# Windowed attention and a mixture of experts on one core: chunks of 4, 6, 7 and 7 tiles instead of four batches of 6, and a first attention written anew

## The chip, the cores and the metric

The kernel runs on one NeuronCore of a Trainium2 chip. The metric is the device time of one execution in microseconds (us); the kernel before takes 1218.8 us (median of three runs). The core has five engines that run side by side, each with its own queue in order: TensorE (PE) multiplies matrices into PSUM, VectorE (DVE) and ScalarE (ACT) work on elements, GpSimd (POOL) too but without access to PSUM, and SyncE (SP) issues most transfers (DMA). They wait for each other through semaphores.

## The reference

Attention for 4 batches, 8 heads, 768 positions and 64 numbers per head, and then a mixture of 4 experts over the 3072 rows, each weighted by a row's probability for it:

```
pos = np.arange(S); rel = pos[:, None] - pos[None, :]
is_global = pos[None, :] < n_global                 # 8
is_local = (rel >= 0) & (rel < n_local)             # 96
dist = np.where(is_global & ~is_local, float(n_local), np.abs(rel))
scores = q @ k.T / sqrt(D) - slopes[:, None, None] * dist
scores = np.where(is_global | is_local, scores, -1e9)
a = np.exp(scores - scores.max(-1)); a /= a.sum(-1) + 1e-9
x = (a @ v).transpose(0, 2, 1, 3).reshape(B * S, H * D)      # 3072 x 512
p = probs / (probs.sum(-1) + 1e-9)
out = sum(p[:, e:e+1] * (np.maximum(x @ w1[e], 0) @ w2[e]) for e in range(4))
```

w1[e] is 512 x 1024 and w2[e] is 1024 x 512. A query needs only the 95 keys before its own, its own, and the first eight.

## The kernel before

A tile is 128 rows of a batch, so a batch has six. Heads go in pairs, since two heads of 64 numbers fill 128 partitions; "a tile-pair" below is one tile for one pair of heads, and there are 96. The window of a tile is 256 keys: 96 of the tile before, 32 at the front of the batch, and its own 128. The first tile of a batch needs its own 128 alone.

**Attention.** `load` fetches q, k and v of a pair with both heads side by side. PE transposes q and k (`transpose_half`: three tiles into PSUM tile `pt`); copies bring them to SBUF. `windows` makes `vg`, v shifted to the windows' first halves. A step then takes one tile-pair a stage further (`flow`): `scores` (two matmuls, one for each head, into `ps`); `softmax`, where DVE adds the bias `nbias` and finds the maximum in one instruction (in profiles CUSTOM_DVE_ANT_0), ACT takes the exponential with the sum `zsum`, and the weights `pb` are scaled by 1/`zsum`; `turn`, where PE transposes `pb` into `pt` and ACT copies it to `pT`; and, for three tiles at once, `weigh`, where PE multiplies with v and vg, head j into 64 rows of `px`, and ACT copies `px` to `x`.

There are two forms of it. The first batch has nothing beside it (`early=True`): q lies in `early_q` with the other head's rows filled with zeros, so that a score matmul uses all 128 rows, in full float32. Later batches run beside the experts: q is split into a high and a low part (`st_q`), laid out by DMA into `qd`, k likewise into `kd`, and two fp32r matmuls per head give the scores.

**Experts.** They run batch by batch, and in a batch by unit: expert e and a quarter g of its 1024 hidden columns, 16 units to a batch. `first(i)` makes the hidden part `h` by Strassen's scheme in Winograd's form: seven products of half-size blocks, which need the blocks and sums B11, B21, B22, T1 to T4 of x (`blocks`; `xB` and `xT` in profiles) and the blocks and sums of w1 (`w1s`). Every operand is a high and a low part, so a product is six matmuls of half a batch's rows, 384 columns. `second(i)` multiplies each tile of `h` with `w2s`, six matmuls of 512 columns, and DVE adds the result, times the row's probability, to `acc`. PSUM tiles of both are `pm`, of which there are four.

**Weights.** Unit i's `raw1` and `raw2` are loaded by SP, POOL makes four sums, ACT copies the high parts and POOL subtracts for the low ones (`load_w1`, `load_w2`). One buffer each for `raw1`, `raw2` and `sums`, two for `w1s` and `w2s`. In the first batch they are also written to memory (`keep`), and in later batches fetched from there (`fetch`).

**Order.** The main loop emits `first(0)`, `first(1)`, `second(0)`, `first(2)`, and so on. After each product or tile it takes a step of the waiting `chores` (the weights of unit i+2, the blocks of the next batch) and as many steps of the next batch's attention as keep it evenly spread. While `Ordered.on` is set, each engine keeps the order of the code; that holds for the first attention and the first seven products. Later a scheduler in the build chooses each engine's order. The first attention is spread in the same way with the weights of units 0 and 1, and with half of the blocks of x (`blocks(0, (0,), po)`).

## Time and profile before

| What | us |
|---|---|
| runs of the kernel | 1215.73 to 1218.8, median 1218.8 |
| span of the profiled execution | 1215.1 |
| PE busy | 1176.1 |
| DVE busy | 824.0 |
| ACT busy | 499.9 |
| POOL busy | 214.1 |
| first matmul of the experts begins | 81.20 |

The profile gives no time of its own for the profiled execution beside its span, so sums are made against 1215.1, which is by the lower of the three runs. The page's slices show how the span divides (40 slices of 30 us; busy tenths, and the granted clock of PE in tenths):

```profile
PE   6789999999999999999999999999999999999997
DVE  5667657767668776766768766676676766666664
ACT  4874556555642453444442344444443211111110
POOL 5465565465541000000002000000000100000000
PEclk9989999999999999999999999999999999999999
```

POOL is busy for the first 380 us, in the first attention and while the weights are split. All recorded calls pass one helper, so every row has the line L42: read them by the names of the tiles. PE and PEld are two rows of one engine, the matmuls and the loads of their stationary operand; recorded times of successive matmuls overlap, so the price of one is read from start to start.

### The profile page before, as it was taken

The page shows a single profiled execution, that of the slowest core. Times are in us where ns is not written, and L with a number is a line of the kernel's source. Part 1 is how long each engine was busy: PE and PEld are TensorE (multiplying, and loading weights), DVE is VectorE, ACT ScalarE, POOL GpSimd, SP SyncE. Part 2 cuts the span into 40 slices and gives each one's busy share as a digit, 9 for nine tenths or more (in the row PEclk, how much of TensorE's full clock was granted, in tenths as well). Part 3 has the DMA queues.
Part 4 walks back from the last instruction along what each step waited for, and adds up shares of the span by engine and source line. Part 5 has one row for each costly group of instructions (what it writes and reads, how often), then busy time and mean ns, then how long its engine had stood idle before and what let it go on. Part 6 is the DMA issues. An engine that isn't in the chain of part 4 may idle for free.

```text
span 1215.1 us, 18027 instructions
## 1 busy us (share of the span) xinstructions
PE 1176.1 (97%) x6624; PEld 1053.3 (87%) x6624; DVE 824.0 (68%) x1778; ACT 499.9 (41%) x1284; POOL 214.1 (18%) x226
## 2 busy tenths in 40 slices
PE   6789999999999999999999999999999999999997
PEld 4568788998998899899898999899899899999996
DVE  5667657767668776766768766676676766666664
ACT  4874556555642453444442344444443211111110
POOL 5465565465541000000002000000000100000000
PEclk9989999999999999999999999999999999999999
DMA  6427978778777757575646856665663655555532
GB/s 161 123 107 218 306 241 275 263 246 308 261 281 251 226 183 225 193 223 199 216 155 218 275 189 205 211 202 192 204 205 142 238 195 191 186 181 182 184 128 88
DMA packets 122705, 251.40 MB, mean 207 GB/s; under 512 B 83184, under 2 KB 91376, under 8 KB 106224
## 3 DMA queue, kind: packets, MB, share of 16 engines
q1 hardware_dynamic: 118864, 243.87, 60.3%
q10 hardware_dynamic: 3744, 6.30, 1.4%
q8 instruction: 54, 0.88, 0.3%
q14 instruction: 43, 0.35, 0.1%
HBM read 174.11 MB, written 52.43 MB: 186 GB/s over the span
## 4 chain that ended last, share of the span: by engine, by line
PE 86%; ACT 4%; DMA 3%; DVE 3%; POOL 2%; issue 2%; SPq 0%; ACTq 0%; POOLq 0%; DVEq 0%
PE pm L42 76%; PE pt L42 6%; PE ps L42 3%; ACT pb L42 2%; DMA raw<-in_moe_w_dram 2%; POOL sums L42 1%; POOL w2s L42 1%; DVE pb L42 1%; PE px L42 1%; DMA qd<-st_q 1%; SPq L42 0%; ACT pT L42 0%; DVE early_q L42 0%; ACT xT L42 0%; DVE x L42 0%
## 5 line engine op out<-in xcount | busy, mean ns | idle before, releaser
L42 PE MATMUL pm<-w2s,h 128*128 128x512 f32 x2304 | 551.6, 393 | 4.5 <-DVE h L42 4.4
L42 PEld LDWEIGHTS pm<-w2s,h 128*128 128x128 f32 x2304 | 426.0, 188 | 92.5 <-DVE h L42 6.5
L42 DVE SCALAR_TENSOR_TENSOR acc<-pm,prob,acc 128x512 f32<-128x512 f32 x360 | 268.1, 749 | 148.7 <-PE pm L42 146.5
L42 PE MATMUL pm<-xT,w1s 128*128 128x384 f32 x1536 | 296.5, 338 | 0.2 <-ACT xT L42 0.2
L42 PEld LDWEIGHTS pm<-xT,w1s 128*128 128x128 f32 x1536 | 267.7, 189 | 2.3 <-issue 1.4
L42 PE MATMUL pm<-xB,w1s 128*128 128x384 f32 x1152 | 226.7, 338 | 1.8 <-DVE xB L42 1.5
L42 PEld LDWEIGHTS pm<-xB,w1s 128*128 128x128 f32 x1152 | 201.2, 188 | 7.0 <-DVE xB L42 1.9
L42 ACT ACTIVATE h<-pm 128x384 fp32r<-128x384 f32 x256 | 124.7, 490 | 178.0 <-DVE pm L42 174.7
L42 DVE SCALAR_TENSOR_TENSOR h<-pm,h 128x384 fp32r<-128x384 f32 x256 | 140.7, 552 | 13.3 <-ACT h L42 9.8
L42 ACT ACTIVATE pb<-pb,nmax 128x256 f32<-128x256 f32 (+1 forms) x192 | 93.1, 487 | 108.2 <-DVE nmax L42 107.5
L42 ACT COPY p<-pm 128x384 f32<-128x384 f32 x64 | 30.6, 477 | 190.8 <-PE pm L42 190.6
L42 POOL COPY vg<-v 32x768 f32<-32x768 f32 x16 | 13.1, 821 | 498.4 <-DMA v<-in_v_dram 495.6
L42 DVE TENSOR_TENSOR u<-pm,p 128x384 f32<-128x384 f32 x64 | 35.6, 556 | 73.7 <-PE pm L42 55.0
L42 ACT ACTIVATE pb<-pb,zsum 128x256 f32<-128x256 f32 (+1 forms) x168 | 74.8, 484 | 18.1 <-DVE zsum L42 18.1
L42 DVE CUSTOM_DVE_ANT_0 pb<-ps,nbias 128x256 f32<-128x256 f32 (+1 forms) x192 | 71.4, 395 | 9.0 <-PE ps L42 4.4
L42 ACT COPY pT<-pt 128x512 f32<-128x512 f32 (+1 forms) x96 | 52.4, 546 | 56.6 <-PE pt L42 56.4
L42 DVE TENSOR_TENSOR pm<-pm,vv 128x384 f32<-128x384 f32 x128 | 71.6, 559 | 1.6 <-PE pm L42 1.4
L42 PE MATMUL pt<-ident,pb 128*128 128x128 f32 x352 | 58.6, 280 | 12.7 <-ACT pb L42 6.3
L42 PEld LDWEIGHTS pt<-ident,pb 128*128 128x128 f32 x352 | 43.3, 143 | 23.1 <-ACT pb L42 14.3
L42 DVE TENSOR_TENSOR vv<-pm,u 128x384 f32<-128x384 f32 x64 | 35.6, 557 | 27.3 <-PE pm L42 26.5
L42 DVE TENSOR_TENSOR u<-pm,u 128x384 f32<-128x384 f32 x64 | 35.6, 557 | 25.3 <-PE pm L42 24.6
L42 POOL TENSOR_TENSOR w2s<-raw,w2s 128x512 fp32r<-128x512 f32 x32 | 41.0, 1295 | 57.9 <-ACT w2s L42 57.7
(88 smaller groups left out, 895.7 us busy)
## 6 DMA issues: line engine op xcount, KB each, us to landing
w1s<-kept SPq DMA_DIRECT2D x48, 1792.0 KB, 7.2
w2s<-kept SPq DMA_DIRECT2D x48, 1024.0 KB, 4.8
kept<-w1s SPq DMA_DIRECT2D x16, 1792.0 KB, 9.6
qd<-st_q SPq DMA_DIRECT2D x96, 192.0 KB, 4.8
raw<-in_moe_w_dram SPq DMA_DIRECT2D x32, 512.0 KB, 5.9
kept<-w2s SPq DMA_DIRECT2D x16, 1024.0 KB, 6.8
v<-in_v_dram SPq DMA_DIRECT2D x16, 384.0 KB, 3.6
out_dram<-acc ACTq DMA_DIRECT2D x24, 256.0 KB, 3.3
```

What stands on the lines that cost most here:

```text
L42: ins = fn(*args, **kwargs)
```

## The change

The 24 tiles of all batches are cut into chunks of 4, 6, 7 and 7 (`SIZES`), and experts and attention go by chunk. A chunk's attention is done in segments that do not cross a batch and have at most four tiles: one of 4; 2 and 4; 2, 4 and 1; 1, 4 and 2. A segment that begins within a batch also loads and turns the tile of keys before it and tile 0 (`tiles_of_keys`), in shorter runs and so in more transfers. The seven products of a unit have 256, 384, 448 and 448 columns. Weights are split in chunks 0 and 1 (`KEEP = 1`), written to memory in chunk 1 and fetched in chunks 2 and 3.

The first attention (four tiles of four pairs, 16 steps instead of 24) is written by itself. q stays without zeros, and a head's score matmul uses its own 64 rows. Scores of two tiles are made together. `pb` is not scaled: the eight sums of a pair stay in PSUM (`z`), DVE makes `zr` = 1/(z + 1e-9), PE turns it by eight small matmuls (`pt<-ident,zr`) and spreads it over 64 rows each, ACT copies that to `rT`, and DVE multiplies the products with v by it when it takes them out of PSUM. The copies to `pT` go from ACT to DVE, the copies of q to ACT alone; k goes to ACT for the first pair and to DVE later. The blocks of x are made in two parts in a new order (`raw_first`), and unit 0 takes its products in that order.

```
+    SIZES = (4, 6, 7, 7)
+    SEG = 4
+    KEEP = 1
+    def tiles_of_keys(t0, t1):
+        return list(range(t1)) if t0 < 2 else [0] + list(range(t0 - 1, t1))
...
+    def first_attention(A):
...
+        def scores(pr, g):
+            ps = A.ps.tile([P, 2, 4 * P], F32, name="ps")
...
+                for j in range(2):
+                    own = slice(j * D, (j + 1) * D)
+                    te.matmul(
+                        ps[:, j, 2 * i * P : 2 * i * P + m],
+                        got["q"][own, t * P : (t + 1) * P],
+                        got["k"].rearrange("p t c -> p (t c)")[own, c0 : c0 + m],
+                        start=True, stop=True,
+                    )
...
+        def sums(pr):
+            zr = A.small.tile([P, SEG, 2], F32, name="zr")
+            ve.tensor_scalar_add(zr, psum[pr]["z"], 1e-9)
+            ve.reciprocal(zr, zr)
+            rt = A.pt.tile([P, 512], F32, name="pt")
+            for i in range(n):
+                for j in range(2):
+                    te.matmul(
+                        rt[j * D : (j + 1) * D, i * P : (i + 1) * P],
+                        zr[:, i, j : j + 1].to_broadcast([P, D]),
+                        ident, start=True, stop=True,
+                    )
+            rT = A.rT.tile([P, 512], F32, name="rT")
+            ac.copy(rT, rt)
...
+        def finish(pr):
+            ve.tensor_mul(x[:, pr, :], psum[pr]["px"], psum[pr]["rT"])
...
+        for s in range(last + 3):
+            m, t = divmod(s, n)
+            if s <= last:
+                softmax(steps[s])
...
+            if t == 0 and m:
+                sums(PAIRS[m - 1])
+            if 1 <= s <= last + 1:
+                turn(A, steps[s - 1], ve.tensor_copy)
+            if s >= 2:
+                weigh(psum[steps[s - 2]["pr"]]["px"], steps[s - 2])
+                if t == 1 and m:
+                    finish(PAIRS[m - 1])
+            if m < NPAIR:
+                if t == 0:
+                    scores(PAIRS[m], 1)
+                if m + 1 < NPAIR:
+                    if t == 0:
+                        prepare_q(PAIRS[m + 1])
+                    if t == 1:
+                        prepare_k(PAIRS[m + 1], ve.tensor_copy)
+                    if t == 2:
+                        scores(PAIRS[m + 1], 0)
+                if t == 2 and m + 2 < NPAIR:
+                    start(PAIRS[m + 2])
...
-        if b > 0:
+        if c > KEEP:
             wts[(i, 1)] = fetch("w1s", (e, g, 1), [P, 2, 7, 2, P], lambda t: {
...
-        waiting[(i, 1)] = (e, g, 1), dst
+        if c == KEEP:
+            waiting[(i, 1)] = (e, g, 1), dst
...
-                chores.append(load_w1(i + 2, 9) if fn is first else load_w2(i + 2))
+                chores.append(load_w1(i + 2, 6) if fn is first else load_w2(i + 2))
```

PE in the first attention, before, from the end of the first three tiles of a pair (`ps` scores, `pt<-ident,pb` the turned weights, `px` products with v):

```order
L42 MATMUL pt<-ident,pb 128x128 x4
L42 MATMUL px<-pT,v 64x128 x2
L42 MATMUL px<-pT,vg 64x128 x2
L42 MATMUL px<-pT,v 64x128 x2
L42 MATMUL px<-pT,vg 64x128 x2
L42 MATMUL px<-pT,v 64x128 x2
L42 MATMUL pt<-ident,q 128x128 x3
L42 MATMUL ps<-early_k,early_q_165 128x256 x2
L42 MATMUL pt<-ident,pb 128x128 x4
```

The same place now, around the end of the first pair:

```order
L42 MATMUL pt<-ident,pb 128x128 x4
L42 MATMUL px<-pT,vg 64x128 x2
L42 MATMUL px<-pT,v 64x128 x2
L42 MATMUL pt<-ident,zr 64x128 x8
L42 MATMUL pt<-ident,pb 128x128 x4
L42 MATMUL px<-pT,vg 64x128 x2
L42 MATMUL px<-pT,v 64x128 x2
L42 MATMUL ps<-early_k,early_q 128x256 x4
L42 MATMUL pt<-ident,q 128x128 x4
L42 MATMUL pt<-ident,pb 128x128 x2
```

Products with v now stand in every step, between transposes, and the turned sums stand among them once for each pair.

DVE in a step of the first attention, before (ISA is the reduction with the bias):

```order
L42 ISA pb,nmax<-ps,nbias 128x256
L42 ISA nmax 128x1
L42 TENSOR_SCALAR zsum<-zsum 128x2
L42 ISA pb,nmax<-ps,nbias 128x256
L42 ISA nmax 128x1
L42 RECIPROCAL zsum<-zsum 128x2
L42 TENSOR_SCALAR pb<-pb,zsum 128x256
L42 COPY early_k<-pt 128x3x128
```

And now, where a pair ends, with its sums and its final multiplication:

```order
L42 TENSOR_SCALAR zr<-z 128x8
L42 RECIPROCAL zr<-zr 128x8
L42 COPY pT<-pt 128x512
L42 ISA pb,nmax<-ps,nbias 128x256
L42 ISA nmax 128x1
L42 ISA pb,nmax<-ps,nbias 128x256
L42 ISA nmax 128x1
L42 COPY pT<-pt 128x256
L42 TENSOR_TENSOR x<-px,rT 128x512
L42 COPY early_k<-pt 128x4x128
```

The scaling is gone from the steps, and the copy of `pT` has come to DVE.

SP beside the first experts, before (one round of loads; `qd` lays out q, `kept` writes split weights):

```order
L42 DMA raw2_1656<-in_moe_w2_dram 128x2x512
L42 DMA raw1_1693<-in_moe_w1_dram 128x4x256
L42 DMA q_1719<-in_q_dram 128x6x64 x2
L42 DMA k_1722<-in_k_dram 128x6x64 x2
L42 DMA kept_1_0_1_1759<-w1s_1597 128x3584
L42 DMA qd_1802<-st_q_1799 64x768 x4
L42 DMA kept_0_3_2_1895<-w2s_1560 128x2048
```

And now, in chunk 0:

```order
L42 DMA q_1540<-in_q_dram 128x2x64 x2
L42 DMA qd_1353<-st_q_1350 64x512 x4
L42 DMA k_1543<-in_k_dram 128x64 x2
L42 DMA k_1543<-in_k_dram 128x3x64 x2
L42 DMA raw1_1587<-in_moe_w1_dram 128x4x256
L42 DMA raw2_1598<-in_moe_w2_dram 128x2x512
L42 DMA v_1301<-in_v_dram 128x64 x2
L42 DMA v_1301<-in_v_dram 128x3x64 x2
L42 DMA vg_1450<-v_1301 96x512
```

The writes of weights are gone from here, and the loads of k and v are twice as many.

More of the change, by code (lines that the diff above doesn't have):

```diff
@@ L321, in transpose_half, with load @@
-    def transpose_half(A, nat, hf):
+    def load(A, src, b, pr, name, tiles, engine=None):
+        runs = []
+        for s, t in enumerate(tiles):
+            if runs and runs[-1][1] + runs[-1][2] == t:
+                runs[-1][2] += 1
+            else:
+                runs.append([s, t, 1])
+        if src is v:
+            nat = A.natv.tile([P, 2, SEG, D], F32, name=name)
+        else:
+            nat = A.nat.tile([P, SEG, 2, D], F32, name=name)
+        for s, t, n in runs:
+            for j in range(2):
+                rows = src[b, 2 * pr + j].rearrange("(t p) d -> p t d", p=P)[:, t : t + n]
+                dst = nat[:, j, s : s + n, :] if src is v else nat[:, s : s + n, j, :]
+                (engine or sy).dma_start(dst, rows)
+        return nat
@@ new lines, in softmax @@
+        def softmax(new):
+            t, i, pr = new["t"], new["i"], new["pr"]
+            cols, bcol, pcol = columns(t)
+            if i == 0:
+                psum[pr] = {
+                    "z": A.pz.tile([P, SEG, 2], F32, name="z"),
+                    "px": A.px.tile([P, 512], F32, name="px"),
+                }
+            z = psum[pr]["z"]
+            nmax = A.small.tile([P, 2], F32, name="nmax")
+            new["pb"] = A.pb.tile([P, 2, 2 * P], F32, name="pb")
+            for j in range(2):
+                e = new["pb"][:, j, pcol]
+                ve.tensor_tensor_reduce(
+                    e, new["ps"][:, j, t % 2 * 2 * P + cols.start : t % 2 * 2 * P + cols.stop],
+                    nbias[:, 2 * pr + j, bcol], 1.0, 3.0e38, ALU.add, ALU.min, nmax[:, j : j + 1],
+                )
+                ac.activation(e, e, AF.Exp, bias=nmax[:, j : j + 1], scale=-1.0, accum_out=z[:, i, j : j + 1])
@@ new lines, in prepare_q @@
+    def prepare_q(A, nat, half, n, got):
+        tp = transposes(A, nat, 2 * half, n)
+        st = A.st.tile([P, 2, 2 * P], F32R, name="st_q")
+        hi, lo = st[:, 0, : n * P], st[:, 1, : n * P]
+        ac.activation(hi, tp[:, : n * P], AF.Copy, scale=-SCALE)
+        ve.scalar_tensor_tensor(lo, tp[:, : n * P], -SCALE, f32(hi), op0=ALU.mult, op1=ALU.subtract)
+        qd = got[("q", half)] = A.qd.tile([P, 2, 2, 2 * P], F32R, name="qd")
+        for j in range(2):
+            for m in range(2):
+                sy.dma_start(f32(qd[m * D : (m + 1) * D, j, :, : n * P]), f32(st[j * D : (j + 1) * D, :, : n * P]))
@@ L482, in flow @@
             if new:
-                new["ps"] = scores(A, new["t"], gots[new["pr"]], early)
+                scores(new)
             if four:
                 turned.append(four)
-            ready = len(turned) == TPH
-            if ready and not early:
-                weigh(A, turned, x)
-            if three and not early:
-                turn(A, three)
-            softmax(A, one, two)
-            if three and early:
-                turn(A, three)
-            if ready and early:
-                weigh(A, turned, x)
@@ new lines, in flow, with start @@
+            if three:
+                turn(A, three, ac.copy)
+            softmax(one, two)
+            tiles[:] = [new, one, two, three]
+        parts, x0 = [], 0
+        for b, t0, t1 in segments(c):
+            parts += [(b, t0, t1, pr, x0) for pr in PAIRS]
+            x0 += (t1 - t0) * P
+        def start(part):
+            b, t0, t1, pr, _ = part
+            ks = tiles_of_keys(t0, t1)
+            return {
+                "q": load(A, q, b, pr, "q", range(t0, t1)),
+                "k": load(A, k, b, pr, "k", ks),
+                "v": load(A, v, b, pr, "v", ks),
+            }
@@ L635, in attn_moe_kernel @@
     NPR = FF // (2 * P)
-    units = [(b, e, g) for b in range(B) for e in range(E) for g in range(NPR)]
+    per = E * NPR
+    units = [(c, e, g) for c in range(len(SIZES)) for e in range(E) for g in range(NPR)]
     wts = {}
@@ L713, in load_w2 @@
             yield 1
-        waiting[(i, 2)] = (e, g, 2), dst
+        if c == KEEP:
+            waiting[(i, 2)] = (e, g, 2), dst
     hs = {}
-    def product(i, a, x):
-        pm = ps_mm.tile([P, 512], F32, name="pm")
-        m = 0
-        for kt in range(2):
-            for wi, xi in ((0, 0), (1, 0), (0, 1)):
-                te.matmul(
-                    pm[:, :HALF], wts[(i, 1)][a][:, wi, kt, :], xb[x][:, xi, kt, :], start=(m == 0), stop=(m == 5)
-                )
-                m += 1
-        return pm
     late = []
```

588 lines of the change are left out of this document (304 added, 284 removed).

## The prediction

> **What bounds the kernel now.** I read the page first, then stretches of the span by engine, then TensorE (PE) in order of time.
>
> ```profile
> span 1215.1 us, 18027 instructions
> PE 1176.1 (97%) x6624; PEld 1053.3 (87%) x6624; DVE 824.0 (68%) x1778; ACT 499.9 (41%) x1284; POOL 214.1 (18%) x226
> PE 86%; ACT 4%; DMA 3%; DVE 3%; POOL 2%; issue 2%; SPq 0%; ACTq 0%; POOLq 0%; DVEq 0%
> ...
> 11.30:81.00 69.70, 56.91 (x398) 44.31 (x397) 44.50 (x191) 57.28 (x175) 33.56 (x36) 0.90 0.35 95
> 93.00:380.00 287.00, 279.85 (x1609) 251.27 (x1608) 197.30 (x427) 157.98 (x395) 150.36 (x150) 1.00 0.78 263
> 350.00:400.00 50.00, 49.63 (x269) 44.68 (x266) 40.76 (x65) 16.38 (x31) 13.21 (x10) 1.00 0.78 256
> 380.00:670.00 290.00, 289.96 (x1666) 261.80 (x1665) 203.03 (x431) 119.55 (x311) 8.75 (x7) 1.00 0.65 209
> ```
>
> The last four rows are stretches: length, busy us of PE, weight loads, DVE, ACT and POOL, then the granted clock. The first is the first attention: no engine is full, ACT is nearest (57.28 of 69.70). From 93 us on PE is busy without a gap worth naming (289.96 of 290.00). So two things set the time: when the experts begin, and how much PE work follows.
>
> ```profile
> 81.20 0.79 PE L42 MATMUL pm<-xB,w1s 128*128 128x384 f32 x3
> 93.06 1.20 PE L42 MATMUL pm<-xB,w1s 128*128 128x384 f32 x6
> 1106.89 3.28 PE L42 MATMUL pm<-xT,w1s 128*128 128x384 f32 x18
> 1110.01 2.24 PE L42 MATMUL pm<-xB,w1s 128*128 128x384 f32 x12
> 129.08 0.64 PE L42 MATMUL ps<-kd,qd 128*128 128x256 f32 x4
> 129.55 1.55 PE L42 MATMUL pm<-w2s,h 128*128 128x512 f32 x6
> 130.94 1.23 PE L42 MATMUL pm<-xB,w1s 128*128 128x384 f32 x6
> ```
>
> Start to start these rows give the price of one matmul: 3.12/18 = 0.173 us at 384 columns, 0.47/4 = 0.118 at 256, 1.39/6 = 0.232 at 512. A straight line through the first two gives 0.200 at 448. The first expert unit is done at 93.06; less its 42 x 0.173 = 7.3 us of work, the experts begin in effect at 85.8.
>
> **Part 1, chunk sizes.** 42 products per unit and 16 units per chunk: before 4 x 672 x 0.173 = 465 us; now 672 x (0.118 + 0.173 + 2 x 0.200) = 464. The second products are the same 2304. So the experts cost PE the same; the ends for 448 columns are 0.173 and 0.232, which I keep as -8 and +10 us after weighing that four points lie on one line. The weight-load rows speak against 256 columns: each load is recorded with a mean of 188 ns (groups by form), longer than 118. If a load could not be shorter, each product of the first chunk would cost at least the 0.173 seen at 384 and the chunk 37 us more; but the four score matmuls at 129.08 have a load each, and took 0.118.
> The Trainium skill (Trainium Kernel Development and Optimization, Performance Expectations) judges the distance to the limit by the busy share of weight loads. Read so, 87% would leave the narrow products little to gain, and the sum would be 37 us higher. The rows at 129.08 do not bear that out here.
>
> **Part 2, attention beside the experts.** 20 tiles are now done there instead of 18, so 80 tile-pairs instead of 72, in 8 segments for each of 4 pairs instead of 3. The order of the built program has 232 transposes of q and k tiles (96 and 136) against 192, and 32 of them instead of 48 in the first attention: 200 beside the experts against 144.
>
> ```profile
> 133.05 0.60 PE L42 MATMUL pt<-ident,pb 128*128 128x128 f32 x4
> 133.40 0.77 PE L42 MATMUL pm<-xT,w1s 128*128 128x384 f32 x3
> 155.46 0.49 PE L42 MATMUL pt<-ident,q 128*128 128x128 f32 x3
> 155.79 0.60 PE L42 MATMUL pt<-ident,pb 128*128 128x128 f32 x4
> 24.79 0.39 PE L42 MATMUL px<-pT,vg 128*64 128x128 f32 x4
> 25.01 0.39 PE L42 MATMUL px<-pT,v 128*64 128x128 f32 x4
> ```
>
> A row of four px matmuls is one window of one tile-pair, both heads side by side in columns (a product in full float32 is recorded twice). A tile-pair costs PE 0.47 (scores) + 0.35 (four transposes) + 2 x 0.22 (products with v) = 1.26 us, a transpose of q or k 0.33/3 = 0.11. So 8 x 1.26 + 56 x 0.11 = +16 us; since seven tiles instead of six now fall in the last chunk, which has no attention beside it, I take 14 (ends 11 and 20).
>
> **Part 3, the first attention.** 16 steps instead of 24. The step before, from the first and the last reduction over scores:
>
> ```profile
> 7.84 0.89 DVE L42 TENSOR_SCALAR nbias<-dist 128x128 bf16<-128x128 f32 x2
> 10.06 2.90 PE L42 MATMUL ps<-early_k,early_q 128*128 128x128 f32 x8 [3.25 <-DVE early_k L42]
> 11.30 0.29 DVE L42 CUSTOM_DVE_ANT_0 pb<-ps,nbias 128x128 f32<-128x128 f32 x1 [1.38 <-PE ps L42]
> 74.72 0.41 DVE L42 CUSTOM_DVE_ANT_0 pb<-ps,nbias 128x256 f32<-128x256 f32 x1
> L42 ACT ACTIVATE pb<-pb,nmax 128x256 f32<-128x256 f32 x160 | 80.5, 505 | 78.4 <-DVE nmax L42 77.8
> L42 ACT COPY pT<-pt 128x512 f32<-128x512 f32 x80 | 46.6, 583 | 55.7 <-PE pt L42 55.5
> L42 ACT CAST w1s<-sums 128x512 fp32r<-128x512 f32 x32 | 19.7, 619 | 16.6 <-POOL sums L42 16.5
> L42 DVE COPY early_k<-pt 128x384 f32<-128x384 f32 x8 | 4.4, 552 | 1.7 <-PE pt L42 1.6
> L42 DVE SCALAR_TENSOR_TENSOR acc<-pm,prob,acc 128x512 f32<-128x512 f32 x360 | 268.1, 749 | 148.7 <-PE pm L42 146.5
> 18.06 1.03 PE L42 MATMUL ps<-early_k,early_q 128*128 128x256 f32 x4
> 18.93 0.60 PE L42 MATMUL pt<-ident,pb 128*128 128x128 f32 x4
> 25.77 0.31 PEld L42 LDWEIGHTS pt<-ident,q 128*128 128x128 f32 x3 [0.17 <-issue]
> ```
>
> 63.4 us over 23 steps: 2.76 each. New work per step of one tile-pair: ACT two exponentials (1.0), a quarter each of the q copy and of the copy of the turned sums (0.58 each): 1.3, and with the casts of weights and blocks, about 18 of 0.4 to 0.6 over 16 steps, 1.85. The two scalings (one on ACT, one on DVE) are gone; the copy pT moves from ACT to DVE. DVE: reductions 0.8, pT 0.72 (0.552 scaled to 512 columns), and a quarter of the k copy, of the final multiplication (0.75 at most, as for acc) and the two operations on sums: 1.9. PE: transposes 0.44 and 0.22, products with v 0.38, sums turned by eight small matmuls 0.22, and scores: two heads took 0.87 on all rows; on half the rows each they take between that and half, if they run together. That is 1.6 to 2.1. PE also changes array shape more often: products with v came three tiles at a time, now each step; the weight load waited 0.17 us where a run ended (25.77), and at two to three changes a step 0.2 to 0.4 is added. All three engines lie at 1.85 to 2.3; before, ACT's own 57.28 of 69.70 was 82%, so I take 2.4 (ends 2.0 and 2.8).
> The Trainium skill (TensorEngine Tiling, Key Properties) says that a change of tiling mode drains TensorE and that different tiles run in parallel. By the first half a step would be nearer 2.8 (+6 us), by the second nearer 2.1; the 0.17 us at 25.77 agrees in kind with the first, and no row here has two heads on half the rows.
> The start: DVE had its bias ready at 8.7 but the first scores waited until 10.06 for the k copy on DVE, behind bias work. That copy is now on ACT and the zeroing of q is gone, so I set the first reduction at 9.0. The loads of the third pair now follow 1 MB of weights by two steps, and the copy of its first keys stands on POOL behind four sums that wait for these weights; I add 2 us. Last reduction 9.0 + 15 x 2.4 + 2 = 47. After it two exponentials, transposes, copy, products and the final multiplication are some 5 us, and the seven products of the first unit 8 us, since each wants a block that ACT and DVE or POOL make one after the other. So the first unit ends at 60 (ends 54 and 67); less its 5.0 us of PE work, experts begin in effect at 55.0. Gain 85.8 - 55.0 = 30.8 us.
>
> **Part 4, the weights of the first chunk.** Chunks 0 and 1 both split the weights; nothing is written to memory in chunk 0. What a unit needs from POOL and ACT stays, while PE's time per unit falls from 287/16 = 17.9 to 5.0 + 24 x 0.232 + (24 x 1.26 + 56 x 0.11)/16 = 12.9 us.
>
> ```profile
> L42 POOL TENSOR_TENSOR w1s<-sums,w1s 128x512 fp32r<-128x512 f32 x28 | 36.4, 1322 | 0.0
> L42 POOL TENSOR_TENSOR w2s<-raw,w2s 128x512 fp32r<-128x512 f32 x30 | 38.4, 1296 | 56.9 <-ACT w2s L42 56.8
> L42 POOL TENSOR_TENSOR sums<-raw 128x256 f32<-128x256 f32 x28 | 20.1, 739 | 60.5 <-DMA raw<-in_moe_w_dram 60.5
> raw<-in_moe_w_dram SPq DMA_DIRECT2D x32, 512.0 KB, 5.9
> SPq L42 <- POOL w2s L42: 69.6, 11, 12.1
> 217.97 2.39 SPq L42 DMA_DIRECT2D qd<-st_q  x4
> ```
>
> POOL per unit: three of 1.3, one of 0.74 and four sums of 0.74 for w1, two of 1.3 for w2: 10.2 us, 79% of 12.9. ACT goes from 158 us in chunk 0 to about 155 (narrower copies, more q and k parts), 75% of 206; DVE from 197 to about 153, 74% (32 accumulations of 0.75 fewer, and 176 results narrower by 128 columns at 0.12, the two reductions' difference above). DVE at 82% in 350:400 cost PE 0.4 us, so shares of this size can be carried. POOL waited 60.5 us over 14 units, 4.3 each, for raw weights: there is one buffer, refilled in 5.9 us once POOL has read it. Then POOL has 2 x 1.32 + 2 x 1.30 = 5.2 us of other work, so the shortest cycle is 10.2 + 0.7 to 1.3, about 11.5 us. SP issues 152 transfers in this chunk at 0.6 us, 91 of 206 us, in order, and waits for POOL in between. All this fits in 12.9, barely. Before, PE stood idle 287 - 279.85 = 7.2 us here; I take 5 us more (ends -3 and +40). In chunk 1 a unit is as before, in 18.4 us, with 248 transfers instead of some 120 on SP: hidden by the same PE work. At the chunk borders the blocks of x have two times four tiles of PE time to be made in, not two times six; that is within the 5 us.
>
> **Sum.** 1215.1 - 30.8 + 14 + 5 = 1203.3 us of span. The runs took 1215.73 to 1218.8, so the profiled one stands at their low end; on the median I say 1205.
>
> **Rivals.** (a) The weight cycle is longer than a unit. For it: POOL's 4.3 us wait per unit, one raw buffer, SP's waits of up to 12.1 us; against it: it overlaps in the order. Beyond 12.9 us every microsecond costs 16; the change breaks even at a unit of 12.9 + 16.8/16 = 13.9, is slower by 0.3% at 14.2, and if landing and all of POOL's work came one after the other (5.9 + 10.2 = 16.1) the time would be 1205 + 51 - 5 = 1251. I put it at 1216 to 1240. (b) Weight loads bound the 256-column products: 1242. (c) The first attention doesn't get a shorter step, 2.76: 5.4 us later, 1210; PE's mode changes speak for it. (d) The two heads overlap fully and nothing starves: step 2.1, idle as before: 1195.
>
> **Numbers.** The measurement tells changes of about 0.3% (3.7 us) from none: faster means below 1215.1, slower above 1222.5. Chances: forecast 0.50, (a) 0.24, (b) 0.04, (c) 0.12, (d) 0.10. Faster: nearly all of the forecast (0.48), (c) 0.10, (d) 0.10, a little of (a) 0.03: 0.71. Same: 0.02 + 0.02 + 0.07 = 0.11. Slower: the rest of (a) and (b): 0.18. The range 1190 to 1228 leaves out the far part of (a), (b), and a very short step; the forecast's own is 1195 to 1214.
>
> **What would show it.** First unit done near 60 us; reductions 2.4 us apart; score matmuls of two heads starting together. Products at 256 and 448 columns 0.118 and 0.200 apart. Chunk 0 about 210 us long, PE idle about 12 us in it, POOL busy near 79%; if instead POOL's wait before sums stays and PE waits for w1s, it is (a). PE work from then on +14. I am wrong if chunk 0 lasts over 225 us or the first unit ends after 70.

## The result, and the profile after

The changed kernel takes 1234.76 us (median of four runs, 1234.49 to 1237.85), the kernel before beside it 1217.64 (1215.73 to 1218.8): a ratio of 1.0147, 95% interval 1.0129 to 1.0166. It is slower, where 1205 was forecast. The profiled execution took 1234.65 us, with a span of 1232.8 against the 1203.3 of the sum: 29.5 us are to be found.

From the page of the changed kernel, and then its four chunks as stretches (length; busy us of PE, weight loads, DVE, ACT and POOL; granted clock, DMA share, GB/s):

```profile
PE 1189.8 (97%) x6728; PEld 1038.6 (84%) x6728; DVE 840.0 (68%) x1785; ACT 549.0 (45%) x1401; POOL 381.4 (31%) x402
57.75:289.60 231.85, 220.02 (x1480) 196.01 (x1479) 167.34 (x420) 158.13 (x420) 176.30 (x178) 0.96 0.53 147
289.60:595.50 305.90, 300.06 (x1739) 268.71 (x1738) 216.00 (x472) 175.12 (x446) 154.74 (x155) 0.99 0.78 260
595.50:938.30 342.80, 340.59 (x1842) 293.93 (x1841) 236.89 (x488) 141.65 (x363) 13.20 (x15) 1.00 0.62 194
938.30:1227.20 288.90, 288.90 (x1345) 252.18 (x1343) 187.23 (x288) 43.42 (x80) 0.00 (x0) 1.00 0.42 151
```

The experts begin early, as meant. But the first chunk lasts 232 us and not 210: PE is idle for 11.8 us of it and the clock is 0.96. The same stretches of the kernel before, chunk by chunk:

```profile
81.20:382.70 301.50, 292.38 (x1663) 261.91 (x1662) 208.22 (x443) 162.79 (x406) 155.28 (x155) 0.99 0.78 265
382.70:670.80 288.10, 288.06 (x1658) 260.21 (x1657) 201.80 (x428) 119.55 (x311) 8.75 (x7) 1.00 0.64 209
959.00:1207.20 248.20, 248.18 (x1249) 224.75 (x1247) 163.31 (x272) 39.15 (x80) 0.00 (x0) 1.00 0.48 174
```

A chunk without attention beside it costs 248.2 us at six tiles and 288.9 at seven, 41.3 a tile in both, at full clock. What differs is what stands beside the products.

Now PE in order of time, in the changed kernel, from the first attention (rows of the timeline; the last bracket is the idle time before the row and what ended it):

```profile
18.31 1.09 PE L42 MATMUL pt<-ident,zr 128*64 128x128 f32 x16 [1.02 <-DVE zr L42]
20.51 1.13 PE L42 MATMUL ps<-early_k,early_q 64*128 64x256 f32 x8
28.75 1.09 PE L42 MATMUL pt<-ident,zr 128*64 128x128 f32 x16 [1.02 <-DVE zr L42]
43.37 1.98 PE L42 MATMUL pt<-ident,zr 128*64 128x128 f32 x16 [5.50 <-DVE zr L42]
57.75 0.86 PE L42 MATMUL pm<-xB,w1s 128*128 128x256 f32 x5
65.27 1.75 PE L42 MATMUL pm<-xT,w1s 128*128 128x256 f32 x12 [2.53 <-DVE u L42]
282.57 7.21 PE L42 MATMUL pm<-w2s,h 128*128 128x512 f32 x18 [4.03 <-DVE acc L42]
300.82 1.31 PE L42 MATMUL pm<-xB,w1s 128*128 128x384 f32 x6 [3.73 <-DVE h L42]
```

The first expert product starts at 57.75 instead of 81.20 us, and the first unit is done at 67.0 instead of 93.2. From there on the waits are few, but long. What stood behind the two at the first chunk border (DVE and ACT):

```profile
279.85 2.00 DVE L42 TENSOR_TENSOR x<-x 128x768 f32<-128x768 f32 x1 [5.35 <-POOL xB L42]
298.64 1.14 ACT L42 CAST w2s<-raw 128x512 fp32r<-128x512 f32 x2 [7.23 <-DMA raw<-in_moe_w_dram]
300.20 0.56 DVE L42 SCALAR_TENSOR_TENSOR h<-pm,h 128x384 fp32r<-128x384 f32 x1 [4.60 <-ACT h L42]
```

DVE, working in order, waits 5.35 us for a rest of a block that POOL makes behind the sums of weights, with the accumulations queued behind it. ACT waits 7.23 us for raw weights, with the relu of `h` behind it. Each time PE runs dry some microseconds later.

**An account from the first unit's end to the last matmul.** For each matmul I take the time from its start to the next one's start; the part after its (modelled) end is idle time, the rest is its own. The last matmul itself, 0.4 us, is in no row. Sums in us, profiled executions:

| | before | after | difference |
|---|---|---|---|
| first expert unit done at | 93.2 | 67.0 | -26.2 |
| PE idle after that | 7.8 | 16.9 | +9.1 |
| attention matmuls | 106.5 | 125.0 | +18.5 |
| expert matmuls at the median of their kind | 982.8 | 988.2 | +5.4 |
| expert matmuls over 1.5 times the median: the excess | 2.8 | 16.2 | +13.4 |
| expert matmuls, other excess | 13.7 | 13.4 | -0.3 |
| behind the last matmul | 7.9 | 5.6 | -2.3 |
| span | 1215.1 | 1232.8 | +17.7 |

The medians are 0.120 us at 256 columns, 0.1735 at 384, 0.2025 at 448 and 0.2275 at 512. The two rows of excess depend on where the line between them is drawn (at 1.4 to 1.75 times the median, the slow ones differ by 10.6 to 13.4 us); their sum doesn't. Cut by place, the sum is firmer: 8.6 us lie wholly or in part at a granted clock of 0.5, where the kernel before has none; 17.1 against 11.9 at full clock, at expert matmuls next to one of the attention; 4.0 against 4.6 inside runs of products. Of the 16.2 us of slow expert matmuls, 8.3 are among those at half clock, right after the waits:

```profile
282.50:289.00 6.50, 6.43 (x16) 5.05 (x17) 6.50 (x9) 2.09 (x4) 6.10 (x6) 0.53 0.65 257
302.00:306.00 4.00, 4.00 (x16) 4.00 (x15) 1.98 (x5) 2.37 (x6) 3.65 (x4) 0.57 0.68 234
```

### The profile page after: what moved, and what is told of

Its sections match the earlier page's. It is cut to its first block, busy times and chain, and to the rows that moved or that the text cites. A ratio compares the mean times of both kernels' runs of the same rounds, so it can differ in the third digit from the quotient of the medians.

```text
span 1232.8 us, 19188 instructions
## 1 busy us (share of the span) xinstructions
PE 1189.8 (97%) x6728; PEld 1038.6 (84%) x6728; DVE 840.0 (68%) x1785; ACT 549.0 (45%) x1401; POOL 381.4 (31%) x402
## 4 chain that ended last, share of the span: by engine, by line
PE 48%; DMA 2%; DVE 1%; ACT 0%; POOL 0%; SPq 0%; issue 0%; DVEq 0%; ACTq 0%
PE pm L42 44%; PE pt L42 2%; DMA qd<-st_q 1%; PE ps L42 1%; DVE acc L42 0%; DMA out_dram<-acc 0%; DMA k<-in_k_dram 0%; POOL xB L42 0%; SPq L42 0%; DVE x L42 0%; DVE h L42 0%; DVE xT L42 0%; ACT xT L42 0%; DVE pm L42 0%; ACT h L42 0%
## 5 line engine op out<-in xcount | busy, mean ns | idle before, releaser
L42 PE MATMUL pm<-xT,w1s 128*128 128x448 f32 (+2 forms) x1536 | 301.6, 342 | 2.5 <-DVE u L42 2.5
L42 PE MATMUL pm<-xB,w1s 128*128 128x448 f32 (+2 forms) x1152 | 230.4, 342 | 4.1 <-DVE h L42 3.7
L42 ACT ACTIVATE h<-pm 128x448 fp32r<-128x448 f32 (+2 forms) x256 | 123.9, 491 | 175.6 <-DVE pm L42 172.4
L42 DVE SCALAR_TENSOR_TENSOR h<-pm,h 128x448 fp32r<-128x448 f32 (+2 forms) x256 | 140.1, 551 | 19.2 <-ACT h L42 15.2
L42 POOL TENSOR_TENSOR w2s<-raw,w2s 128x512 fp32r<-128x512 f32 x64 | 82.6, 1307 | 74.7 <-ACT w2s L42 74.3
L42 POOL TENSOR_TENSOR w1s<-sums,w1s 128x512 fp32r<-128x512 f32 x64 | 82.5, 1307 | 9.5 <-ACT w1s L42 9.1
L42 POOL TENSOR_TENSOR w1s<-raw,w1s 128x512 fp32r<-128x512 f32 x64 | 65.0, 1030 | 45.8 <-ACT w1s L42 45.1
L42 DVE TENSOR_TENSOR u<-pm,p 128x448 f32<-128x448 f32 (+2 forms) x64 | 35.7, 557 | 62.3 <-PE pm L42 49.3
L42 DVE TENSOR_TENSOR pm<-pm,vv 128x448 f32<-128x448 f32 (+2 forms) x128 | 71.6, 559 | 5.2 <-PE pm L42 4.1
L42 POOL TENSOR_TENSOR sums<-raw 128x256 f32<-128x256 f32 x64 | 47.2, 755 | 37.2 <-DMA raw<-in_moe_w_dram 36.9
```

Source lines behind the costliest of these rows:

```text
L42: ins = fn(*args, **kwargs)
```

## The experiments

Four theories were open. (1) In the first attention and at the borders, engines that work in order wait for block work or transfers that stand behind something else. (2) The weights, split in two chunks now, need POOL and ACT for longer than a unit lasts. (3) The added attention work on PE. (4) The first attention itself. Each ratio is to the kernel before, run beside it.

### The blocks of the first chunk on DVE

```diff
-                chores.append(blocks(0, (0,), po, True))
+                chores.append(blocks(0, (0,), ve, True))
```

> Edit of the changed kernel: in the first attention four rests of the first two row blocks of x are subtracted on VectorE (DVE) instead of GpSimd (POOL). Theory 1 (an engine working in order waits for block work that stands on POOL behind the sums of weights): DVE's two waits near 40 us shrink, the reductions of the third pair come earlier, PE's wait of 5.5 us at 43.4 falls below 3, and the first product starts at 53 to 55 instead of 57.75: 3 to 5 us less in all. Theory 4 (the step itself is too long, whoever makes the blocks): DVE has four more operations of about half a microsecond, nothing is gained, 0 to +2 us.

1235.25 us, 1.0135 [1.0114, 1.0156]: no change. The wait for the third pair's sums is 5.57 us instead of 5.50, and the first unit ends at 67.2. The rests that stayed on POOL, and the casts between, hold DVE as long. Theory 1 is not borne out at this place.

### The border blocks on DVE

```diff
-        rest(po, "B22", b22)
+        rest(low, "B22", b22)
...
-        rest(po, "T3", b12)
+        rest(low, "T3", b12)
...
-        rest(po, "B21", b21)
+        rest(low, "B21", b21)
```

> Edit of the changed kernel: the three rests of the blocks of x that POOL makes at each chunk border (B22, T3, B21) are subtracted on DVE. Theory 1: PE's 8.9 us of idle time between 270 and 310 us falls to 3 or 4, and a little is won at the two later borders: 6 to 10 us less in all. Theories 2 and 3 (the weights' cycle through POOL and ACT, or the added attention work, are what costs): less than 2 us.

1230.11 us, 1.0101 [1.0073, 1.0128]. The border in the changed kernel, and in this one:

```profile
270.00:310.00 40.00, 31.14 (x139) 27.52 (x137) 26.91 (x47) 15.17 (x35) 28.92 (x24) 0.87 0.65 227
270.00:310.00 40.00, 35.45 (x181) 31.41 (x182) 37.46 (x66) 21.29 (x52) 31.46 (x28) 1.00 0.76 258
```

PE is busy for 4.3 us more, the clock stays at 1.00, and 42 more matmuls fit in. The span falls by 5.7 us (the median by 4.7), just under the low end of what theory 1 said: chunk 0 is 7.4 us shorter, chunk 1 2.1, but chunk 2 is 3.2 longer, by a new wait of 2.5 us for keys at its border. So theory 1 holds for 5 to 6 of the 29.5 us.

### The weights written in chunk 0, split once

```diff
-    KEEP = 1
+    KEEP = 0
```

> Edit of the changed kernel: the split weights are written to memory in chunk 0 and read back in chunks 1, 2 and 3, so chunk 1 no longer splits them (one part of the change undone). Theory 2 (splitting the weights costs in both chunks): chunk 1 shrinks from 306 to about 297 us and the first border loses most of its idle time; chunk 0 gets 16 x 2.3 MB of writes and grows by 0 to 4; 8 to 14 us less in all. Theory 3 (added attention work): within 3 us of the changed kernel. Theory 1 alone: the border gains some 5 us, since POOL has no sums ahead of the blocks.

1316.2 us, 1.0800 [1.0777, 1.0822]: 81 us more, where all theories had the same or less. Chunk 0, chunk 1, and what PE waited for longest:

```profile
57.20:378.80 321.60, 251.84 (x1475) 213.00 (x1474) 167.06 (x419) 154.50 (x407) 155.26 (x157) 0.87 0.71 245
378.80:682.20 303.40, 301.15 (x1750) 266.70 (x1749) 213.73 (x476) 137.55 (x366) 14.54 (x16) 1.00 0.70 221
PE pm L42 <- POOL w1s L42: 25.8, 19, 3.2
```

With the write in it (2.8 MB a unit, w1s and w2s, not the 2.3 expected) the weight cycle is 20 us a unit (321.6/16), and PE waits for it: idle 70 us, clock 0.87. This is what rival (a) described; in the changed kernel itself PE never waited for split weights by a row of the waits. Chunk 1, now without splitting, is 303.4 us: 2.5 less than in the changed kernel. Its idle time falls from 5.8 to 2.3 us and it has no half clock, but its other matmuls take more. The second splitting costs chunk 1 little in all.

### No splitting after the first two units

```diff
-        if c > KEEP:
-            wts[(i, 1)] = fetch("w1s", (e, g, 1), [P, 2, 7, 2, P], lambda t: {
+        if i > 1:
+            wts[(i, 1)] = fetch("w1s", (0, i % 2, 1), [P, 2, 7, 2, P], lambda t: {
```

(and so for the second weights, with `KEEP = 0`; the kernel leaves out the later units' own weights, they use those of the first two)

> Edit of the changed kernel that leaves out work: only the weights of the first two units are split; every later unit reads these back from memory, in chunks 0 and 1 too (so the weights of later units are not the ones they should be). PE's work is unchanged; POOL and ACT lose nearly all weight work in chunks 0 and 1. Theory 2: chunk 0 falls from 232 to 210 to 214 us, chunk 1 from 306 to 297, in all 25 to 30 us less, 1205 to 1210. Theory 3: chunk 0 stays above 225 and the total loses less than 8 us. Theory 1: only the border (270 to 310 us) gains, 5 to 9 us, because POOL is free to make the blocks.

1242.57 us, 1.0195 [1.0173, 1.0216]: not 25 us less but 8 more. POOL is busy for 16 us of chunk 0 instead of 176, and it lasts 242.1 us.

```profile
57.70:299.80 242.10, 218.71 (x1475) 190.22 (x1474) 160.00 (x419) 110.38 (x323) 16.05 (x17) 0.98 0.80 267
124.05 1.19 PE L42 MATMUL pm<-w2s,h 128*128 128x512 f32 x2 [11.24 <-DMA w2s<-kept]
```

One wait of 11.24 us for weights read back, and the slow clock after it (2 us), explain the difference to 229; that is still 19 us over the prediction's 210. So theory 2 is not borne out: with hardly any work for POOL, chunk 0 is no faster. The test is not clean, since reading split weights back in units of 13 us brings waits of its own.

### All block work on DVE; the second unit's weights later; the attention later

All are built on the kernel with the border blocks on DVE. The first moves every rest of the first chunk's blocks to DVE too, the second and third are the edits below, and the fourth has both of these:

```diff
-            if n == 9:
+            if n == 13:
                 chores.append(load_w1(1, lead=2, hold=3))
```

```diff
-        begin = ONSTEPS if c == 0 else 0
+        begin = ONSTEPS + 6 if c == 0 else 6
...
+                if c > 0 and done == 1:
+                    next(att, None)
```

> The kernel with the border blocks on DVE, with every rest of the first chunk's blocks on DVE too, so that no block work is left on POOL. Theory 1 (the wait of 5.5 us for the third pair's sums comes from rests on POOL behind the sums of weights): the wait falls below 2.5, the first product starts near 54 to 55 us, the total is 3 to 4 us below the 1230.1 of the kernel it is built on. Rival (the chain of casts on ACT and subtractions on DVE holds the reductions back wherever the rests are made): the wait stays above 4 and the total is within 2 us of 1230.

1233.92 us, 1.0145 [1.0128, 1.0162]. The wait for sums grew to 6.59 us and the first unit ends at 70.9. The wait is as the rival said; the total, 3.8 above 1230.1, is worse than either had it.

> The kernel with the border blocks on DVE, with the load of the second unit's first weights put four steps later in the first attention, so that POOL meets the first blocks' rests before these sums. Theory 1: the wait of 5.5 us falls below 3 and the first product starts near 55; the total is 2 to 4 us below 1230.1. Rival: the second unit's weights are late instead, PE waits for w1s after the first unit, and the total is the same or up to 4 us above.

1230.69 us, 1.0115 [1.009, 1.0141], as the kernel it is built on. The wait fell from 5.50 to 3.18 us and the first product starts 4 us earlier, but the unit is done at 66.3 us, only 1 us before that of the kernel it is built on:

```profile
53.93 0.85 PE L42 MATMUL pm<-xB,w1s 128*128 128x256 f32 x5
63.37 2.93 PE L42 MATMUL pm<-xT,w1s 128*128 128x256 f32 x12 [2.83 <-DVE u L42]
66.10 1.48 PE L42 MATMUL pm<-xB,w1s 128*128 128x256 f32 x6
```

The seven products now take 12.4 us instead of 9.3. PE waits 2.83 us for `u`, which stands in DVE's queue behind the making of blocks, and the 12 products behind that wait take 2.7 us from start to start, 1.6 in the changed kernel: they lie at half clock. So of the wait of 5.5 us, the longest before the experts, little could be had back this way; that the making of the blocks holds the unit's end is read from the rows and was not tested apart. Neither theory had that: PE did not wait for the second unit's weights either.

> The kernel with the border blocks on DVE, with the attention of the next chunk begun six steps later in each chunk: its loads are still asked for at once, but its first transposes and scores come after more expert work. Theory 1 (PE, which works in order, waits at the start of a chunk for transfers and for split keys that were asked for just before): the stalls near 74 us (1.9 and 1.1) and near 594 us (2.5) and the half clock after them go, 4 to 8 us below the 1230.1 of the kernel it is built on. Theory 3 (added PE work): within 2 us of 1230.

1231.44 us, 1.0116 [1.0095, 1.0137]: the same, without the 4 to 8 us of theory 1. The waits near 594 us are gone, those near 74 are down to 1.3 us; a new one of 3.42 us stands at 151 and one of 2.24 near 575.

> The last kernel with, besides, the second unit's first weights loaded four steps later in the first attention. Theory 1: the wait for the third pair's sums (5.5 to 3.2 us) goes without the stalls that took its place, 1222 to 1226. Rival (the blocks of x for the first unit set its end wherever PE waits): as the last kernel within 1.5 us.

1233.6 us, 1.0126 [1.0104, 1.0148]: nothing gained either, with a wait of 4.63 us back at the first border. Waits taken away one by one come up elsewhere.

### The two parts of the first attention undone

For the first, `sums` and its matmuls go, and each step has:

```diff
+            ve.tensor_scalar_add(z[:, i], z[:, i], 1e-9)
+            ve.reciprocal(z[:, i], z[:, i])
+            ve.tensor_scalar_mul(p[:, 0, pcol], p[:, 0, pcol], z[:, i, 0:1])
+            ac.activation(p[:, 1, pcol], p[:, 1, pcol], AF.Copy, scale=z[:, i, 1:2])
```

> Edit of the changed kernel that undoes one part of the first attention: each probability is multiplied by 1/sum before its transposition, as before the change (one scaling on DVE, one on ACT for each step, and the two small operations on the sums each step), and the eight small matmuls that turn the sums for each pair, their copy and the multiplication of the products go away. If the step is set by ACT and DVE: a pair takes 11 to 12 us instead of 10.4, the first product starts at 60 to 62, the total rises by 2 to 5 us. If it is set by PE and its wait for the sums (1.0 us of wait and 1.1 to 2.0 of matmuls for each pair): a pair takes 9 to 10, the first product starts at 53 to 55, the total falls by 3 to 5.

1255.23 us, 1.0306 [1.0284, 1.0328]. The first product starts at 81.9 us, 24 later; a step takes 4.33 us. PE waits 26 us for `pb` (19.5 of it for DVE, 6.3 for ACT), and the clock from 10 us on is 0.74:

```profile
PE pt L42 <- DVE pb L42: 19.5, 14, 3.4
10.00:81.90 71.90, 46.06 (x248) 28.74 (x244) 38.55 (x140) 33.02 (x103) 32.06 (x37) 0.74 0.31 79
```

In this order of work the scaling of a step stands behind the reductions of the next one and ahead of its own transposition. No engine is busy for more than 65% of the stretch, so the loss is a chain and not a load. The size was not foreseen. It is not the price of the scaling in the kernel before, whose step took 2.76 us with it.

For the second:

```diff
-                        got["q"][own, t * P : (t + 1) * P],
-                        got["k"].rearrange("p t c -> p (t c)")[own, c0 : c0 + m],
+                        got["q"][:, j, t * P : (t + 1) * P],
+                        got["k"].rearrange("p t c -> p (t c)")[:, c0 : c0 + m],
```

> Edit of the changed kernel that undoes the other part: the scores of a head are made on all 128 rows with q set to zero on the other head's half, as before the change (the zeroing is done once on POOL, the scaling of q is one operation on ACT and one on DVE for each pair). Two tile-pairs of scores then cost PE about 1.74 us instead of the 1.06 seen. If PE is on the path in the first attention: a pair takes 11.5 to 12 us instead of 10.4, the first product starts at 61 to 63 and the total rises by 4 to 5. If not: less than 1.5 us.

1245.05 us, 1.0231 [1.0214, 1.0248]. The first product starts at 69.6 us, 11.9 later, of which the scores' own time makes 5.4 (16 x 0.34); a step takes 3.48 us and the clock there is 0.83 (0.93 in the changed kernel). PE is on the path in the first attention, but the loss is over twice what was expected for that. The clock is a part of it, and the scores are not all that changed: q is scaled partly on DVE now, and PE waits 2.4 us for that.

### The second splitting alone, in the kernel before

```diff
-        if b > 0:
+        if b > 1:
```

(for both weights; they are written in chunk 1, whose loads are asked for after six steps instead of nine)

> Edit of the kernel before: the weights are split in the first two chunks instead of the first alone (written to memory in chunk 1), with chunks of 6 tiles and the old first attention; the loads of chunk 1's raw weights are asked for six steps after a unit begins, as in the changed kernel. Theory 2 (the second splitting costs): 5 to 15 us above the kernel before. Theories 1 and 3: within 0.3%, since a unit of 18 us hides a weight cycle of 12 us.

1219.76 us, 1.0017 [1.0006, 1.0028]: within 0.3%, as theories 1 and 3 had it. But not because it is hidden. Chunk 0 falls from 301.5 to 296.1 us and chunk 1 grows from 288.1 to 298.0, with a wait at the border that the kernel before doesn't have:

```profile
385.31 4.21 PE L42 MATMUL pm<-xB,w1s 128*128 128x384 f32 x12 [5.20 <-ACT p L42]
381.42 1.14 ACT L42 CAST w2s<-raw 128x512 fp32r<-128x512 f32 x2 [12.28 <-DMA out_dram<-acc]
```

ACT stands 12.28 us ahead of the same cast of raw weights as in the changed kernel (put down here to an output transfer), with six tiles to cover it. And the kernel that splits once, narrow first chunk and all, has no gap over 0.5 us in the 50 us behind its first border. So this border wait, the second of the two above, comes with splitting weights there and doesn't need the narrow chunk. The kernel that splits once has units of 20 us ahead of its border, so that half of the comparison is the weaker one.

### The price of a stall, by itself

```diff
             add(u, product("S2", "T2"), p1)
+            for _ in range({50: 8, 53: 16, 56: 24, 59: 32}.get(i, 0)):
+                ve.tensor_scalar_mul(u, u, 1.0)
```

> Edit of the changed kernel that measures the price of a stall by itself: in four units of the last chunk, which has no idle time of its own and a full clock, 8, 16, 24 and 32 multiplications of u by one are put on DVE behind the first sum of the unit, so that PE runs out of free result buffers and waits. If a stall costs its length alone: the last chunk grows from 288.9 us by the sum of the stalls. If a stall of some microseconds also costs granted clock (theory 1's second half): after the longer stalls the clock is 0.5 for 3.5 to 7 us, and the chunk grows by the sum of the stalls and 1.7 to 3.4 us for each of these; the short stalls, under some 1 to 2 us, cost their length alone.

1264.05 us, 1.0380 [1.0359, 1.0402]. The last chunk grew from 288.9 to 316.4 us, by 27.5; PE's idle time in it is 19.4, and the other 8.1 lie in slower matmuls. The rows: the stretch after two stalls of 0.4 and 0.5 us; two stalls as PE shows them; the stretch after 1.14 and 1.62 us close together; after 1.14 and 5.04 (the fourth stall, 1.14 and 8.47, is not shown):

```profile
975.00:1020.00 45.00, 44.28 (x203) 38.11 (x204) 30.85 (x49) 7.28 (x14) 0.00 (x0) 1.00 0.47 169
1034.70 11.29 PE L42 MATMUL pm<-w2s,h 128*128 128x512 f32 x42 [1.62 <-DVE vv L42]
1097.04 12.46 PE L42 MATMUL pm<-w2s,h 128*128 128x512 f32 x42 [5.04 <-DVE vv L42]
1034.00:1038.00 4.00, 3.30 (x8) 2.31 (x9) 3.94 (x8) 1.61 (x3) 0.00 (x0) 0.57 0.95 348
1095.50:1102.50 7.00, 5.46 (x12) 3.97 (x13) 5.88 (x11) 1.61 (x3) 0.00 (x0) 0.51 0.35 150
```

Of the 8.1 us, some 6 lie in the stretches at half clock. Stalls of 0.4 and 0.5 us left the clock alone. From two short ones in 3 us upward, the work behind the stall has a clock near 0.5 for 3 to 5.5 us. So each of these three stalls cost its length and 1.6 to 2.8 us more, the longest 1.8. That the pair of 1.14 and 1.62 would already do it was not expected; the last section shows what it goes by.

### The rewritten first attention alone

The kernel before, with chunks of 6 tiles and everything else as it was, and only its first attention replaced by that of the changed kernel, in halves of three tiles:

```diff
-        A = Pools(start_stack, "start", st=1, kd=2, qd=1, nat=2, natv=3, pb=4, ps=3, pt=4, px=1, early=True)
-        for n, _ in enumerate(attention(0, A, early=True)):
+        A = Pools2(
+            start_stack, "start",
+            dict(kd=2, qd=2, nat=2, natv=3, vg=2, pb=4, pT=4, rT=2, small=4),
+            dict(ps=2, pt=2, px=1, pz=1),
+        )
+        for n, _ in enumerate(first_attention(A)):
```

> The kernel before with one part of the change alone: its first attention rewritten as in the changed kernel (two heads on half the rows each, 1/sum multiplied into the products with v, in halves of three tiles), chunks of 6 tiles and everything else as before. If the rewritten first attention is a gain of its own, and the loss comes from the chunk sizes: 24 steps of 2.5 us instead of 2.76 and a start 1.4 us earlier, less the waits for sums twice as often (8 halves, up to 1 us each): the first product starts at 73 to 77 us instead of 81.2, nothing changes behind it, 1210 to 1214. If the rewriting itself brings stalls and half clock into the experts: first product earlier, but the total within 3 us of the kernel before or above it.

1208.88 us, 0.9928 [0.9915, 0.9942]: the fastest of all, and faster than both. Its span is 1207.0 us. Its chunk 0:

```profile
79.60:376.40 296.80, 291.34 (x1662) 260.45 (x1661) 208.48 (x444) 162.29 (x404) 154.84 (x154) 1.00 0.79 270
```

By the account above: first unit done at 90.8 (2.4 earlier than before, 2.2 of it because the first reduction comes at 9.08 and not at 11.30), idle time 4.9 (2.9 less), attention 106.2, slow expert matmuls 2.9, both as before; 2.5 less behind the last matmul. The total is below the 1210 to 1214 expected, though the first product, at 79.6, came later than the 73 to 77. The gain is real, but does not come from a shorter step, and no run shows why idle time fell. Over the first attention, from the first to the last reduction, a step takes 2.81 us here, 2.76 in the kernel before and 2.77 in the changed kernel:

```profile
9.85 0.29 DVE L42 CUSTOM_DVE_ANT_0 pb<-ps,nbias 128x128 f32<-128x128 f32 x1 [2.36 <-PE ps L42]
51.35 0.42 DVE L42 CUSTOM_DVE_ANT_0 pb<-ps,nbias 128x256 f32<-128x256 f32 x1
9.08 0.29 DVE L42 CUSTOM_DVE_ANT_0 pb<-ps,nbias 128x128 f32<-128x128 f32 x1 [1.26 <-PE ps L42]
73.81 0.42 DVE L42 CUSTOM_DVE_ANT_0 pb<-ps,nbias 128x256 f32<-128x256 f32 x1
```

(the first two rows are the changed kernel's, 41.50/15; the other two this one's, 64.73/23). So the step of the changed kernel against this one is the chunk sizes, with all that they carry with them (the second splitting, the segments, the narrow first chunk, the new order of its blocks; not taken apart further): 1232.8 - 1207.0 = 25.8 us of loss. The rewriting alone is a gain of 8.1.

## Why the prediction was wrong

Four terms of the sum were mis-sized and one was missing.

- **Part 3, the step of the first attention.** 2.4 us a step was taken and 2 us once for the third pair, 38 us from the first reduction to the last; 41.5 were measured, 2.77 a step. An undisturbed pair took 10.44 us (sums at 18.31 and 28.75), 2.61 a step; the next took 14.62. The rows of PE show why: the sums of each pair make it wait 1.0 us and cost it 1.1 to 2.0, and block work in DVE's queue makes one such wait 5.5. The mean is that of rival (c), but by these waits; that changes of array shape did it, as (c) had it, no run shows. That the two heads overlap was right: 8 score matmuls take 1.06 us start to start, 0.53 a tile-pair against 0.87 before. The first reduction came at 9.85 (9.0 said), the last at 51.35 (47), the first product 6.4 us later (5), the seven products of the first unit took 9.3 (8), and the unit ended at 67.0 (60): +7.0 us. Of the 26.2 us gained at the start, 21.9 are eight steps fewer.
- **Part 2, attention beside the experts.** +14 was taken, out of my own sum of 16; +18.5 measured. The reason given for taking off 2 (the last chunk has no attention beside it) was none, since the sum already counted the tile-pairs done beside experts; and a tile-pair with its transposes cost 2.3 us (18.5/8) and not 2.0. +4.5.
- **Part 1, prices.** The narrow products were right in kind: 0.120 and 0.2025 measured, 0.118 and 0.200 taken. So rival (b) is out. Over 630 and 1344 products these differences make 4.6 us, less 1.3 for the products of before (0.1735 against 0.173); by the account it is +3.1 (5.4, of which 2.3 is only that the first unit is shorter).
- **Part 4, idle time.** +5 was taken, for chunk 0; +9.1 was measured after the first unit. In chunk 0 the forecast held: PE was idle for 8.9 us after the first unit against 7.2 before, and for 11.8 with it, where about 12 had been named. The excess lies where nothing was put: chunk 1 was to be hidden by the same PE work, but had 5.8 us of idle time (0.0 before), and chunk 2 had 2.2 (0.6 before). The waits come at single places, where an in-order queue holds block work, a cast or scores behind a load, and shares of busy time don't show them. +4.1. The sentence on the borders looked at PE time to cover them (two times four tiles); the experiments put the second wait there with the splitting of weights in chunk 1, which brings it with six tiles as well.
- **Missing: what a wait does to the clock.** The stretch rows of before showed a clock of 0.90 in the first attention, and I read no price from it. Slow expert matmuls cost +13.4, the largest term of the miss. Of their 16.2 us, 8.3 lie at half clock right after the waits, where the kernel before has none; of the other 8.0, 7.0 are at matmuls next to one of the attention, and that part was not tested apart.

Behind the last matmul 2.3 us went away, as in all kernels with the rewritten first attention; why, no run shows. 7.0 + 4.5 + 3.1 + 4.1 + 13.4 - 0.3 - 2.3 = 29.5.

Of the signs named ahead, "chunk 0 lasts over 225 us" came true (232). The 210 us set for it were too few by the prediction's own unit: 16 x 12.9 us and 12 of idle time make 218. The other 14 us are mostly matmuls at half clock (6.9) and expert matmuls next to those of the attention (some 6). Rival (a) was right that slower is the other side, and its time of 1216 to 1240 holds the result, but not by its mechanism: by no row did PE wait for split weights, and the kernel without splitting was not faster. What is left of it is the border, where ACT stands 7.23 us for raw weights and PE runs dry behind it.

The Trainium skill (Trainium Kernel Development and Optimization, Performance Expectations) takes the busy share of weight loads as a good measure of the distance to the limit. Read as in the prediction, 87% would have meant 37 us more. In chunk 0 weight loads were busy for 196.01 of 231.85 us, and the products still took 0.120 us each: the trace does not agree. The Trainium skill (TensorEngine Tiling (Array Packing), Key Properties) says that different tiles work in parallel and that a change of mode drains the engine. The trace agrees with the first (0.53 us against 0.87). A step near the 2.8 that the prediction drew from the second is what came, but the waits for sums make it up, and no run here shows the second by itself.

Still open is how much of the 13 us of slow matmuls and 9 of idle time a better order of queues could win back beyond the 5 to 6 of the border blocks: four tries moved the waits. Without any idle time or slow matmul the account would leave the changed kernel at 1232.8 - 16.9 - 16.2 = 1199.7 us, the kernel before at 1204.5, and the one with the rewritten first attention alone at 1207.0 - 4.9 - 2.9 = 1199.2. By this estimate the whole change could win 5 us at best, not 12, and the chunk sizes by themselves nothing.

## What to carry to other kernels

Work moved from a serial start to beside a stage that is bound by PE is still paid there: a tile-pair cost 2.8 us of span in the first attention and 2.3 us of PE beside the experts, so the move wins the difference of two prices and not the first of them. Price a wait by its length and by the slow clock behind it, and look for waits at the places where an in-order queue meets a late load, not in shares of busy time. And when a change has two parts, run each alone: here one part was a gain of 0.7%, hidden under a loss of 2%.

## What the runs showed of the hardware that was not expected

- The granted clock of PE was 1.00 or 0.50, and the half clock came in pieces of 3.41 us or a multiple of it, in each run on one grid. It goes by how long PE was busy in the piece before, so not only the length of a wait counts but also where it falls. Over the fifteen traces, from 16 us on and up to the last 8, the half clock followed each of the 51 pieces at full clock in which PE was busy for less than 1.49 us, 27 of 63 with 1.49 to 2.20, and none with more. So a wait of 2.53 us before 65.27 us was followed by half clock in the changed kernel, and one of 2.53 us in the kernel with the border blocks on DVE was not; nor were the single waits of 1.8 to 2.0 us of the kernel before. Piece by piece, the changed kernel and then the other:

```profile
63.38:66.79 3.41, 1.52 (x12) 1.52 (x13) 2.83 (x7) 1.31 (x3) 3.41 (x5) 1.00 0.00 0
66.79:70.20 3.41, 3.41 (x18) 3.41 (x17) 2.21 (x8) 2.73 (x8) 3.41 (x5) 0.50 0.00 0
64.01:67.42 3.41, 1.81 (x15) 1.81 (x16) 2.83 (x8) 1.38 (x4) 3.41 (x6) 1.00 0.00 0
67.42:70.84 3.42, 3.42 (x31) 3.23 (x29) 2.79 (x9) 3.42 (x9) 3.42 (x4) 1.00 0.00 0
```

- Reading 2.8 MB of split weights back in each unit of 13 us brought one wait of 11.2 us, and writing as much made the unit 20 us, at 267 and 245 GB/s; in the 18 us units of the kernel before the same writes go with 9 us of PE idle time in the whole chunk. Whether the transfers themselves or their place in the queues make the difference, no run shows.
- A DVE subtraction of 128x256 took 0.41 us where it began 0.02 us ahead of a POOL operation on weights, which then took 0.99 us (0.72 for one of the same form at 37.90). It took 0.93 where POOL had begun 0.07 us ahead of it. The second of the two waited, by these rows; it was not tested apart.

```profile
36.12 0.41 DVE L42 TENSOR_TENSOR x<-x 128x256 f32<-128x256 f32 x1
36.14 0.99 POOL L42 TENSOR_TENSOR sums<-raw 128x256 f32<-128x256 f32 x1
41.49 0.72 POOL L42 TENSOR_TENSOR xT<-x,xT 128x256 fp32r<-128x256 f32 x1
41.56 0.93 DVE L42 TENSOR_TENSOR x<-x 128x256 f32<-128x256 f32 x1 [0.62 <-POOL xB L42]
```
